# Projecting the output head group by head group, with attention units reordered head-major and mixed anew, in a decode attention kernel

## The chip, the cores and the metric

The kernel runs on one core of one Trainium2 chip. The metric is the device time of one execution in microseconds (us), as the median of several executions. Every kernel was timed in the same rounds, on the same chip, as the kernel before.

Engine names as in the profile: PE does matmuls (PEld loads their weights), DVE, ACT and POOL do elementwise work and reductions, SP issues the loads.

## The reference

Two independent attention layers (A and B), each with one query token per sequence. The outputs are concatenated.

```python
B, Sq, D = 8, 1, 1024
H, Sk, Dh = 32, 4096, 128
q = (x @ wq).reshape(B, Sq, H, Dh).transpose(0, 2, 1, 3)
scores = einsum("bhqd,bhkd->bhqk", q, k_cache) * (Dh ** -0.5)
p = softmax(scores, axis=-1)
o = einsum("bhqk,bhkd->bhqd", p, v_cache)
return o.transpose(0, 2, 1, 3).reshape(B, Sq, H * Dh) @ wo
```

The inputs are bfloat16. K and V of both layers are 1.07 GB; wq and wo add 8 MB each per layer. The scores are small, so the softmax is nearly uniform.

## The kernel before

A "unit" is one (batch, head) pair: 256 per layer, 512 in all, each with 1 MB of K and 1 MB of V. Scores are computed in one of two ways. A **P unit** transposes K on PE, has ACT evict it, and multiplies on PE (QK). A **D unit** multiplies K by the broadcast query on DVE and reduces there. `kinds` gives the mix; before it is "PD", alternating. Softmax and PV are the same for both kinds.

```python
def do_Dmul(u):          # D unit: DVE multiplies 128x4096 by 128x4096, both in SBUF
    m = plan.add("dve", lambda e: e.tensor_tensor(prod, K_sb[:, slot, :], qbc_broadcast, ALU.mult),   # cut
                 deps=[opK[u], opQbc[u], ...])
    opKfree[u] = m       # K's slot is free: SP may issue the load of unit u + 4
# ... cut: do_Dred reduces prod to 128x32 scores on DVE

def do_softmax(u):
    o1 = plan.add("dve", lambda e: e.tensor_reduce(rmax[:, u:u + 1], src, AX.X, ALU.max), deps=[opQK[u]])
    o2 = plan.add("pool", lambda e: e.partition_all_reduce(gmax[:, u:u + 1], rmax[:, u:u + 1], 128, ReduceOp.max), deps=[o1])
    o3 = plan.add("pool", lambda e: e.tensor_scalar(negb[:, u:u + 1], gmax[:, u:u + 1], -scale, None, ALU.mult), deps=[o2])
    o4 = plan.add("act", lambda e: e.activation(pT[:, u % PR, :], src, ACTF.Exp, bias=negb[:, u:u + 1],
                                                scale=scale, accum_out=rsum[:, u:u + 1]), deps=[o3, opPV.get(u - PR)])
    # ... cut: after each 8 units, one all-reduce (add) of their 8 sums on POOL -> Lall

def issue_K(u):          # on SP, in program order; V likewise, three units behind K
    deps = [opKfree.get(u - NK)] if u >= NK else []
    opK[u] = dma(K_sb[:, slot, :], caches[c][1][b, h]..., ("k", slot), deps)

# ... cut: after all 256 units of a layer, do_E1 normalises 128x256 outputs at once, then
# do_proj runs 2 x 32 matmuls (one per head and output half), and do_out stores the result
```

## Time and profile before

Each unit has one POOL all-reduce, which combines the maxima of the 128 partitions (`gmax<-rmax`), and then one small POOL operation that negates and scales the result (`negb<-gmax`), called negb below. The distance between two negb starts is thus the time of one unit.

| reading (profiled run, span 8085.1 us) | value |
|---|---|
| median time | 8086.3 us |
| negb starts, mean distance | 15.64 us, 511 times = 7994 us |
| gap from negb's end to the next all-reduce's start, mean | 7.21 us |
| from an all-reduce's start to its negb, mean (without the first unit) | 8.17 us |
| last negb to the end | 29.7 us |

First, the page: busy time by engine, then the chain that ended last.

```profile
PE 2556.2 (32%) x17812; PEld 1343.7 (17%) x17812; DVE 1790.5 (22%) x1043; ACT 1457.0 (18%) x1857; POOL 582.3 (7%) x1106
...
issue 74%; DVE 12%; POOL 7%; PE 5%; ACT 1%; POOLq 1%; DMA 0%; SPq 0%; DVEq 0%
```

No engine is busy for a third of the span, and three quarters of the chain is "issue", time that waits for nothing the profile shows. The page's groups (line, engine, operation, count, busy us, mean ns, idle time just before them) say whose time it is:

```profile
L406 POOL PARTITION_ALL_REDUCE gmax<-rmax x512 | 338.3, 661 | 3127.2 <-issue 1727.4
L408 POOL TENSOR_SCALAR negb<-gmax 128x1 f32<-128x1 f32 x512 | 133.2, 260 | 3851.0 <-issue 3851.0
```

POOL, 7% busy, stands before these two lines for 3127 + 3851 of 8085 us. The timeline of two units (start us, duration us, engine, line, operation; in brackets the idle time before) shows the rhythm. SPq lines are load issues.

```profile
4015.02 0.26 POOL L408 TENSOR_SCALAR negb<-gmax 128x1 f32<-128x1 f32 x1 [7.47 <-issue]
...
4020.00 0.33 SPq L131 DMA_DIRECT2D V_sb<-in_B_v_cache_dram  x1
...
4021.26 0.38 POOL L406 PARTITION_ALL_REDUCE gmax<-rmax  x1 [5.98 <-issue]
4021.31 2.29 DVE L384 TENSOR_TENSOR prod<-K_sb,qbc 128x4096 bf16<-128x4096 bf16 x1 [15.04 <-ACT qbc L370]
...
4025.11 0.33 SPq L131 DMA_DIRECT2D K_sb<-in_B_k_cache_dram  x1
4025.48 0.43 SPq L131 DMA_DIRECT2D V_sb<-in_B_v_cache_dram  x1
4025.96 0.43 SPq L131 DMA_DIRECT2D K_sb<-in_B_k_cache_dram  x1
4030.67 0.26 POOL L408 TENSOR_SCALAR negb<-gmax 128x1 f32<-128x1 f32 x1 [9.03 <-issue]
...
4038.09 0.38 POOL L406 PARTITION_ALL_REDUCE gmax<-rmax  x1 [7.16 <-DVE rmax L404]
```

All-reduce, 6 to 10 us of nothing, negb, 6 to 10 us of nothing, and so on, 512 times. The row maximum that an all-reduce needs was ready 7 to 28 us before POOL had finished the previous unit, in all but three units, so POOL does not wait for data. The releaser in the last bracket is inferred and is a coincidence: that maximum was not the one this all-reduce needed. POOL's reported spans are thus no measure of the time it takes here: they sum to 7% of the span, the distances between negb starts to 99%.

The projection is at the very end:

```profile
8055.33 0.26 POOL L408 TENSOR_SCALAR negb<-gmax 128x1 f32<-128x1 f32 x1 [6.78 <-issue]
...
8065.12 9.46 PE L489 MATMUL misc<-W_sb,on_sb 128*8 128x512 bf16 x32 [4.12 <-DVE on_sb L475]
...
8075.36 7.07 PE L489 MATMUL misc<-W_sb,on_sb 128*8 128x512 bf16 x32 [0.77 <-DVE orow L497]
8082.46 0.68 DVE L497 CAST orow<-misc 8x512 bf16<-8x512 f32 x1 [7.16 <-PE misc L489]
```

### The profile page before, as it was taken

To read this page: it belongs to the slowest core of one execution; us is meant where nothing else is said; L and a number is where in the kernel's file an instruction comes from. 1 tells how busy PE (TensorE), PEld (TensorE's weight loads), DVE (VectorE), ACT (ScalarE), POOL (GpSimd) and SP (SyncE) were. 2 spreads that over 40 slices of the span, in tenths; PEclk is the share of its full clock that TensorE was granted. 3 is DMA by queue.
4 is the path that set the end of the run, shared out by engine and by line. 5 is a ranking of instruction groups with operands and counts; after the bars stand their busy time and mean duration, and the time that the engine had idled before them with its cause. 6 is when DMAs were issued, how large, how long until landed. Compare 5 with 4: busy or idle time off the path is not lost.

```text
span 8085.1 us, 43421 instructions
## 1 busy us (share of the span) xinstructions
PE 2556.2 (32%) x17812; PEld 1343.7 (17%) x17812; DVE 1790.5 (22%) x1043; ACT 1457.0 (18%) x1857; POOL 582.3 (7%) x1106
## 2 busy tenths in 40 slices
PE   3333333232323232323333233333333333333333
PEld 2111111111111111111111111111111111111111
DVE  2222222222222222222222222222222222222221
ACT  1111111111111111111111111111111111111111
POOL 0000000000000000000000000000000000000000
PEclk6566666666666666666566566665666566666666
DMA  6333333333333333333343333333333333333331
GB/s 271 125 146 125 146 125 146 125 146 125 138 132 138 132 140 131 137 134 131 139 166 131 140 129 142 126 144 126 144 125 146 125 146 125 145 125 145 125 145 63
DMA packets 158470, 1110.20 MB, mean 137 GB/s; under 512 B 16928, under 2 KB 16928, under 8 KB 25152
## 3 DMA queue, kind: packets, MB, share of 16 engines
q1 hardware_dynamic: 158272, 1107.43, 35.3%
q8 instruction: 140, 2.29, 0.1%
q14 instruction: 58, 0.48, 0.0%
HBM read 1107.33 MB, written 0.03 MB: 137 GB/s over the span
## 4 chain that ended last, share of the span: by engine, by line
issue 74%; DVE 12%; POOL 7%; PE 5%; ACT 1%; POOLq 1%; DMA 0%; SPq 0%; DVEq 0%
DVE s_sb L396 10%; PE sc L334 4%; POOL gmax L406 4%; POOL negb L408 2%; POOL Lall L420 1%; ACT pT L410 1%; DVE prod L384 1%; DVE rmax L404 1%; POOLq L408 0%; PE misc L489 0%; DMA W_sb<-in_A_wq_dram 0%; PE misc L206 0%; PE sc L437 0%; POOLq L74 0%; POOLq L406 0%
## 5 line engine op out<-in xcount | busy, mean ns | idle before, releaser
L437 PE MATMUL sc<-V_sb,pT 128*4 128x512 bf16 x4096 | 1484.3, 527 | 4017.7 <-ACT accS L445 4007.6
L437 PEld LDWEIGHTS sc<-V_sb,pT 128*4 128x4 bf16 x4096 | 386.3, 104 | 4899.4 <-ACT accS L445 4160.0
L404 DVE TENSOR_REDUCE rmax<-sc 128x1 f32<-128x32 f32 x256 | 49.0, 191 | 5171.9 <-PE sc L334 5171.9
L396 DVE TENSOR_REDUCE s_sb<-prod 128x32 f32<-128x4096 bf16 x256 | 1128.7, 4409 | 0.5 <-DVE rmax L404 0.5
L311 ACT ACTIVATE KT_sb<-kt_all 128x4096 bf16<-128x4096 bf16 x256 | 917.3, 3583 | 8.5 <-PE kt_all L297 2.3
L334 PE MATMUL sc<-QB,KT_sb 128*128 128x64 bf16 x8192 | 469.0, 238 | 1403.7 <-ACT pT L410 1403.6
L410 ACT ACTIVATE pT<-s_sb,negb 128x32 bf16<-128x32 f32 x256 | 82.2, 321 | 4132.7 <-POOL negb L408 4132.7
L384 DVE TENSOR_TENSOR prod<-K_sb,qbc 128x4096 bf16<-128x4096 bf16 x256 | 585.3, 2286 | 891.5 <-ACT qbc L370 874.4
L334 PEld LDWEIGHTS sc<-QB,KT_sb 128*128 128x128 bf16 x8192 | 429.5, 128 | 1463.6 <-ACT pT L410 1463.6
L406 POOL PARTITION_ALL_REDUCE gmax<-rmax x512 | 338.3, 661 | 3127.2 <-issue 1727.4
L297 PE MATMUL kt_all<-ident,K_sb 128*128 128x128 f32 x4096 | 519.7, 282 | 3.8 <-ACT KT_sb L311 3.8
L410 ACT ACTIVATE pT<-sc,negb 128x32 bf16<-128x32 f32 x256 | 73.5, 287 | 2378.4 <-POOL negb L408 2378.4
L297 PEld LDWEIGHTS kt_all<-ident,K_sb 128*128 128x128 f32 x4096 | 459.4, 145 | 130.9 <-issue 130.9
L408 POOL TENSOR_SCALAR negb<-gmax 128x1 f32<-128x1 f32 x512 | 133.2, 260 | 3851.0 <-issue 3851.0
L445 ACT ACTIVATE accS<-sc 4x512 bf16<-4x512 f32 x512 | 300.4, 587 | 24.7 <-PE sc L437 6.9
L420 POOL PARTITION_ALL_REDUCE Lall<-rsum x64 | 110.9, 1733 | 492.0 <-issue 486.0
L458 PE MATMUL o_ps<-E,accS 128*128 128x4 bf16 x512 | 33.3, 169 | 60.3 <-ACT accS L445 54.0
L404 DVE TENSOR_REDUCE rmax<-s_sb 128x1 f32<-128x32 f32 x256 | 47.6, 186 | 8.9
L410 ACT ACTIVATION_READ_ACCUMULATOR pT<-sc,negb 128x1 f32 x256 | 49.3, 193 | 0.0
L370 ACT ACTIVATE qbc<-misc 128x512 bf16<-128x512 f32 x64 | 38.2, 597 | 58.6 <-PE misc L358 57.1
L410 ACT ACTIVATION_READ_ACCUMULATOR pT<-s_sb,negb 128x1 f32 x256 | 47.6, 186 | 0.0
L458 PEld LDWEIGHTS o_ps<-E,accS 128*128 128x128 bf16 x512 | 22.6, 102 | 132.2 <-ACT accS L445 132.2
(36 smaller groups left out, 156.3 us busy)
## 6 DMA issues: line engine op xcount, KB each, us to landing
K_sb<-in_A_k_cache_dram SPq DMA_DIRECT2D x256, 1024.0 KB, 8.6
V_sb<-in_A_v_cache_dram SPq DMA_DIRECT2D x256, 1024.0 KB, 6.8
K_sb<-in_B_k_cache_dram SPq DMA_DIRECT2D x256, 1024.0 KB, 8.3
V_sb<-in_B_v_cache_dram SPq DMA_DIRECT2D x256, 1024.0 KB, 6.8
W_sb<-in_A_wq_dram SPq DMA_DIRECT2D x8, 1024.0 KB, 12.0
W_sb<-in_B_wq_dram SPq DMA_DIRECT2D x8, 1024.0 KB, 17.0
W_sb<-in_A_wo_dram SPq DMA_DIRECT2D x8, 1024.0 KB, 14.3
W_sb<-in_B_wo_dram SPq DMA_DIRECT2D x8, 1024.0 KB, 14.9
```

The source lines that it names most:

```text
L297: return e.transpose(kt_all[:, g, tt * 128:(tt + 1) * 128], K32[:, slot, tp * 128:(tp + 1) * 128], ident32[:])
L311: return e.activation(KT_sb[:, pi % 2, lo * 1024:hi * 1024], ktb_all[:, lo:hi, :].rearrange("p g c -> p (g c)"), ACTF.Copy)
L334: return e.matmul(bank[:, 2 * tp:2 * tp + MW], KT_sb[:, pi % 2, tp * 256 + e_:(tp + 1) * 256:2], QB[:, c, (j * 2 + e_) * 2:(j * 2 + e_) * ...
L384: lambda e: e.tensor_tensor(prod[:].rearrange("p (t d) -> p t d", d=Dh), K_sb[:, slot, :].rearrange("p (t d) -> p t d", d=Dh), qbc[:, gi % ...
L396: lambda e: e.tensor_reduce(s_sb[:, di % SR, :], prod[:].rearrange("p (t d) -> p t d", d=Dh), AX.X, ALU.add),
L404: o1 = plan.add("dve", lambda e: e.tensor_reduce(rmax[:, u:u + 1], src, AX.X, ALU.max), deps=[opQK[u]], name=f"rmax{u}")
L406: o2 = plan.add("pool", lambda e: e.partition_all_reduce(gmax[:, u:u + 1], rmax[:, u:u + 1], 128, bass.bass_isa.ReduceOp.max), deps=[o1], ...
L408: o3 = plan.add("pool", lambda e: e.tensor_scalar(negb[:, u:u + 1], gmax[:, u:u + 1], -scale, None, ALU.mult), deps=[o2], name=f"negb{u}")
L410: o4 = plan.add("act", lambda e: e.activation(pT[:, u % PR, :], src, ACTF.Exp, bias=negb[:, u:u + 1], scale=scale, accum_out=rsum[:, u:u + ...
L420: o5 = plan.add("pool", lambda e: e.partition_all_reduce(Lall[:, u0:u1], rsum[:, u0:u1], 128, bass.bass_isa.ReduceOp.add), deps=[opExp[uu] ...
L437: return e.matmul(bank[32 * q4:32 * q4 + 4, 0:512], pT[:, u % PR, 4 * g:4 * g + 4], V_sb[:, slot, g * 512:(g + 1) * 512], start=(g == 0), ...
L445: a = plan.add("act", lambda e: e.activation(accS[32 * q4:32 * q4 + 4, ring, :], bank[32 * q4:32 * q4 + 4, 0:512], ACTF.Copy), deps=[op, o ...
```

## The change

The intent was to take the output projection off the end. Units run head by head (all 8 batches of head 0, then head 1), so that a head's outputs are complete early. Each head is normalised on its own, and the projection runs in nine pieces per layer (seven of four heads, one of three, one of one) that are accumulated in SBUF. The same diff also changes the mix of units from "PD" to "PDD", makes the last two units P units, moves the loads of the second wq and of wo to later units and the first computation of q behind the first unit's transposes, and lets the first V loads leave earlier.

```diff
-    kinds_pat = cfg.get("kinds", "PD")
+    kinds_pat = cfg.get("kinds", "PDD")
+    for u in range(max(0, NT - cfg.get("tail_p", 2)), NT):
+        kind[u] = "P"
 # ... cut
         def unit_src(u):
             c, j = divmod(u, N)
-            b, h = divmod(j, H)
+            h, b = divmod(j, B)
 # ... cut: do_E1 (all heads at once) becomes do_HE(c, h), one head
-        def do_proj(c, ph, wo_ops):
-            for h in range(H):
+        def do_piece(c, h0, h1, wo_ops, final):
+            for ph in range(NPH):
+                for h in range(h0, h1):
+                    # matmuls into misc, start at h0, stop at h1 - 1
+                if h0 == 0:   # DVE copies misc to oacc
+                else:         # DVE adds misc to oacc (to orow in the last piece)
 # ... cut: the schedule of q, wo and the pieces
```

More of the change, by code (lines that the diff above doesn't have):

```diff
@@ L43, in _build_kernel @@
     MW = cfg.get("MW", 64)
-    LB = cfg.get("LB", 8)
-    kinds_pat = cfg.get("kinds", "PD")
+    kinds_pat = cfg.get("kinds", "PDD")
     act_banks = cfg.get("act_banks", 4)
@@ L65, in _build_kernel @@
     assert D % PW == 0 and 2 * N <= 512
+    LB = B
     kind = [kinds_pat[u % len(kinds_pat)] for u in range(NT)]
+    for u in range(max(0, NT - cfg.get("tail_p", 2)), NT):
+        kind[u] = "P"
     p_units = [u for u in range(NT) if kind[u] == "P"]
@@ L101, in _build_kernel @@
         pT = sb("pT", [128, PR, T], BF16)
-        rl = sb("rl", [128, N], FP32)
+        rl = sb("rl", [128, 4, B], FP32)
+        oacc = sb("oacc", [B, NC, D], FP32)
         on_sb = sb("on_sb", [128, NC, H, B], BF16)
@@ L216, in q_compute @@
                 "dve",
-                lambda e: e.tensor_copy(
-                    qT_sb[:, c, 0:N].rearrange("p (b h) -> p h b", h=H),
-                    misc[:, 0:N].rearrange("p (h b) -> p h b", b=B)),
+                lambda e: e.tensor_copy(qT_sb[:, c, 0:N], misc[:, 0:N]),
                 deps=[last], name=f"q{c}_evac")
@@ L236, in _build_kernel @@
         op_q = [None] * NC
-        op_q[0] = q_compute(0, wq_ops)
         opKfree = {}
@@ L462, in do_EXT @@
                     deps = [opAcc[uu] for uu in range(u0, u0 + 4)] + [op_E4]
-                    if j == 0 and c > 0:
-                        deps.append(opE1[c - 1])
+                    deps += [v_ for v_ in list(opHE.values())[-2:]]
                 op = plan.add("pe", fn, deps=deps, name=f"EXT{u0}_{jj}")
@@ L467, in do_EXT @@
                 opExt[uu] = op
-        def do_E1(c):
-            u_last = (c + 1) * N - 1
-            a = plan.add("dve", lambda e: e.reciprocal(rl[:, 0:N], Lall[:, c * N:(c + 1) * N]),
-                         deps=[opAradd[uu] for uu in range(c * N, (c + 1) * N, LB)] + [opE1.get(c - 1)], name=f"E1a{c}")
-            b_ = plan.add(
-                "dve",
-                lambda e: e.tensor_tensor(
-                    on_sb[:, c, :, :].rearrange("p h b -> p b h"),
-                    o_ps[:, c * N:(c + 1) * N].rearrange("p (b h) -> p b h", h=H),
-                    rl[:, 0:N].rearrange("p (b h) -> p b h", h=H),
-                    ALU.mult),
-                deps=[a, opExt[u_last]], name=f"E1b{c}")
-            opE1[c] = b_
@@ L483, in _build_kernel @@
-        proj_ops = {}
-        def do_proj(c, ph, wo_ops):
-            last = None
-            for h in range(H):
-                def fn(e, h=h):
-                    return e.matmul(misc[0:B, 0:PW], on_sb[:, c, h, :], W_sb[:, h * D + ph * PW: h * D + (ph + 1) * PW],
-                                    start=(h == 0), stop=(h == H - 1))
-                deps = []
-                if h == 0:
-                    deps = [opE1[c], last_misc_reader[0]] + wo_ops
-                last = plan.add("pe", fn, deps=deps, name=f"P{c}_{ph}_{h}")
-            if ph == NPH - 1:
-                w_last_user[0] = last
-            ev = plan.add("dve", lambda e: e.tensor_copy(orow[0:B, c, ph * PW:(ph + 1) * PW], misc[0:B, 0:PW]),
-                          deps=[last], name=f"Pev{c}_{ph}")
-            last_misc_reader[0] = ev
-            proj_ops[(c, ph)] = ev
-            return ev
+        opHE = {}
@@ new lines, in _build_kernel, with do_HE @@
+        piece_last = {}
+        pieces_done = {c: 0 for c in range(NC)}
+        def do_HE(c, h):
+            u0 = c * N + h * B
+            ring = h % 4
+            a = plan.add("dve", lambda e: e.reciprocal(rl[:, ring, :], Lall[:, u0:u0 + B]),
+                         deps=[opAradd[u0], opHE.get((c, h - 4)) if h >= 4 else None], name=f"HEa{c}_{h}")
+            b_ = plan.add("dve", lambda e: e.tensor_tensor(on_sb[:, c, h, :], o_ps[:, u0:u0 + B], rl[:, ring, :], ALU.mult),
+                          deps=[a, opExt[u0 + B - 1]], name=f"HEb{c}_{h}")
+            opHE[(c, h)] = b_
@@ new lines, in do_piece, with fn @@
+        def do_piece(c, h0, h1, wo_ops, final):
+            for ph in range(NPH):
+                last = None
+                for h in range(h0, h1):
+                    def fn(e, h=h, ph=ph):
+                        return e.matmul(misc[0:B, 0:PW], on_sb[:, c, h, :], W_sb[:, h * D + ph * PW: h * D + (ph + 1) * PW],
+                                        start=(h == h0), stop=(h == h1 - 1))
+                    deps = []
+                    if h == h0:
+                        deps = [opHE[(c, hh)] for hh in range(h0, h1)] + [last_misc_reader[0]] + wo_ops
+                    last = plan.add("pe", fn, deps=deps, name=f"P{c}_{h0}_{ph}_{h}")
+                dst = orow[0:B, c, ph * PW:(ph + 1) * PW] if final else oacc[0:B, c, ph * PW:(ph + 1) * PW]
+                if h0 == 0:
+                    ev = plan.add("dve", lambda e, dst=dst: e.tensor_copy(dst, misc[0:B, 0:PW]),
+                                  deps=[last], name=f"Pev{c}_{h0}_{ph}")
+                else:
+                    ev = plan.add("dve", lambda e, dst=dst, ph=ph: e.tensor_tensor(dst, oacc[0:B, c, ph * PW:(ph + 1) * PW], misc[0:B, 0:PW], ALU.add),
+                                  deps=[last, piece_last.get(c)], name=f"Pev{c}_{h0}_{ph}")
+                last_misc_reader[0] = ev
+                if ph == NPH - 1:
+                    piece_last[c] = ev
+                    if final:
+                        w_last_user[0] = last
+            pieces_done[c] = h1
@@ L503, in do_out @@
         def do_out(c):
-            deps = [proj_ops[(c, ph)] for ph in range(NPH)]
-            return dma(out[:, 0, c * D:(c + 1) * D], orow[0:B, c, :], "o", deps, f"out{c}")
+            return dma(out[:, 0, c * D:(c + 1) * D], orow[0:B, c, :], "o", [piece_last[c]], f"out{c}")
         LAG_V = cfg.get("LAG_V", 3)
@@ L511, in _build_kernel, with piece_sizes @@
         PV_LAG_D = cfg.get("PV_LAG_D", 2)
-        assert SM_LAG_P >= QK_LAG and PV_LAG_P > SM_LAG_P or (PV_LAG_P >= SM_LAG_P)
-        IT_WQ_LOAD = {c: (c - 1) * N + cfg.get("q_load_at", 1) for c in range(1, NC)}
-        IT_Q_COMP = {c: (c - 1) * N + cfg.get("q_comp_at", min(6, N - 3)) for c in range(1, NC)}
-        IT_WO_LOAD = {c: c * N + cfg.get("wo_load_at", min(8, N - 1)) for c in range(NC)}
+        HE_DELAY = cfg.get("he_delay", 2)
+        PC_DELAY = cfg.get("pc_delay", 2)
+        OUT_DELAY = cfg.get("out_delay", min(24, N - 8))
         TAIL = max(PV_LAG_P, PV_LAG_D) + 1
-        IT_PROJ = {c: (c + 1) * N + TAIL for c in range(NC)}
-        for c in range(1, NC):
-            assert IT_WQ_LOAD[c] < IT_Q_COMP[c] < IT_WO_LOAD[c - 1] <= c * N + 1
-        for c in range(1, NC):
-            assert IT_WO_LOAD[c] > IT_PROJ[c - 1] + NPH - 1, (IT_WO_LOAD, IT_PROJ)
+        IT_WQ_LOAD = {c: cfg.get("q_load_at", min(10, max(1, N // 8))) + (c - 1) * cfg.get("q_step", min(24, max(2, N // 4)))
+                      for c in range(1, NC)}
+        IT_Q_COMP = {c: IT_WQ_LOAD[c] + cfg.get("q_comp_dly", min(12, max(1, N // 8))) for c in range(1, NC)}
+        IT_Q_COMP[0] = 0
+        IT_WO_LOAD0 = (max(IT_Q_COMP.values()) + cfg.get("wo_dly", min(12, max(1, N // 8)))) if NC > 1 else 2
+        def piece_sizes():
+            sizes = []
+            rem = H
+            while rem > 5:
+                sizes.append(4)
+                rem -= 4
+            if rem > 1:
+                sizes.append(rem - 1)
+            sizes.append(1)
+            return sizes
+        PSZ = piece_sizes()
+        assert sum(PSZ) == H
         pending_wq = {}
         wo_loaded = {}
-        out_ops = []
+        wo_iter = {}
+        piece_iter_last = {}
+        out_ops = {}
+        out_due = {}
         k_next = 0
         v_next = 0
-        n_iter = NT + TAIL + NPH
+        n_iter = NT + TAIL + 8
         QBC_AHEAD = cfg.get("qbc_ahead", 2)
@@ L531, in _build_kernel @@
         ext_done = 0
-        e1_done = 0
+        ext_iter = {}
+        he_done = {c: 0 for c in range(NC)}
+        he_iter = {}
         for it in range(n_iter):
+            last_it = (it == n_iter - 1)
             progressed = True
@@ L540, in _build_kernel @@
                     progressed = True
-                if v_next < NT and (v_next <= k_next - 1 - LAG_V or k_next >= NT) and (v_next < NV or (v_next - NV) in opPV):
+                vmax = (k_next - 1 - LAG_V) if (k_next < NT and k_next > NK) else NT
+                if v_next < NT and v_next <= vmax and (v_next < NV or (v_next - NV) in opPV):
                     issue_V(v_next)
@@ L548, in _build_kernel @@
             for c in range(NC):
-                if it == IT_WO_LOAD[c]:
-                    wo_loaded[c] = load_wo(c)
+                if c in wo_loaded:
+                    continue
+                ready = all(q is not None for q in op_q) and (c == 0 or (pieces_done[c - 1] == H))
+                if ready and it >= (IT_WO_LOAD0 if c == 0 else 0) and it >= wo_iter.get(c - 1, -100) + 1:
+                    if c == 0 or it >= piece_iter_last[c - 1] + NK + 4 or last_it:
+                        wo_loaded[c] = load_wo(c)
+                        wo_iter[c] = it
             while qbc_done < len(d_units):
@@ L560, in _build_kernel @@
                 do_EXT(ext_done + 3)
+                for uu in range(ext_done, ext_done + 4):
+                    ext_iter[uu] = it
                 ext_done += 4
-            while e1_done < NC and ext_done >= (e1_done + 1) * N and all(uu in opAradd for uu in range(e1_done * N, (e1_done + 1) * N)):
-                do_E1(e1_done)
-                e1_done += 1
+            for c in range(NC):
+                while he_done[c] < H:
+                    h = he_done[c]
+                    u1 = c * N + (h + 1) * B - 1
+                    if u1 >= ext_done or (c * N + h * B) not in opAradd:
+                        break
+                    final_head = (c == NC - 1 and h == H - 1)
+                    if not (final_head or it >= ext_iter[u1] + HE_DELAY or last_it):
+                        break
+                    do_HE(c, h)
+                    he_iter[(c, h)] = it
+                    he_done[c] += 1
+            for c in range(NC):
+                if c not in wo_loaded:
+                    continue
+                while pieces_done[c] < H:
+                    h0 = pieces_done[c]
+                    acc_ = 0
+                    for sz in PSZ:
+                        if acc_ == h0:
+                            break
+                        acc_ += sz
+                    h1 = h0 + sz
+                    if he_done[c] < h1:
+                        break
+                    final = (h1 == H)
+                    last_piece = final and c == NC - 1
+                    if not (last_piece or last_it or (it >= he_iter[(c, h1 - 1)] + PC_DELAY and it >= wo_iter[c] + NK + 6)):
+                        break
+                    do_piece(c, h0, h1, wo_loaded[c], final)
+                    piece_iter_last[c] = it
+                    if final:
+                        out_due[c] = it + (OUT_DELAY if c < NC - 1 else 0)
+            for c in range(NC):
+                if c in out_due and c not in out_ops and (it >= out_due[c] or last_it):
+                    out_ops[c] = do_out(c)
             if it < NT:
@@ L569, in _build_kernel @@
                     do_Dmul(it)
+            for c in range(NC):
+                if it == IT_Q_COMP[c]:
+                    wq_o = wq_ops if c == 0 else pending_wq.pop(c)
+                    op_q[c] = q_compute(c, wq_o)
             u = it - SM_LAG_P
@@ L581, in _build_kernel @@
                     do_PV(u)
-            for c in range(1, NC):
-                if it == IT_Q_COMP[c]:
-                    op_q[c] = q_compute(c, pending_wq.pop(c))
-            for c in range(NC):
-                for ph in range(NPH):
-                    if it == IT_PROJ[c] + ph:
-                        assert c in opE1
-                        do_proj(c, ph, wo_loaded[c])
-                        if ph == NPH - 1:
-                            out_ops.append(do_out(c))
         assert len(out_ops) == NC and k_next == NT and v_next == NT, (len(out_ops), k_next, v_next)
@@ L594, in _build_kernel @@
         assert qbc_done == len(d_units) and ext_done == NT
+        assert all(pieces_done[c] == H for c in range(NC))
         counts = {e: 0 for e in ENGINES}
```

## The prediction

> **What bounds the kernel now.** Not the projection, nor any engine by busy time (page, part 1: PE 32%, DVE 22%, ACT 18%, POOL 7%). In the chain of waits 74% is "issue" under POOL's lines L406 (all-reduce of the maximum) and L408 (negb). In the timeline POOL runs one strict sequence for each of 512 units: all-reduce, 7.2 to 9.3 us later negb, 5.9 to 9.5 us later the next all-reduce. negb starts are 15.64 us apart on average (least 13.3); 511 x 15.64 = 7994 of 8085 us. The row maximum an all-reduce needs was ready 7 to 25 us before POOL had finished the previous unit, in all but 3 units: POOL is never short of work. The instruction listing shows an extra unnamed POOL instruction before nearly every all-reduce and every negb[...].
>
> With no loads in flight (last units) a unit takes 13.3 us. The other 2.3 us are disturbance: K and V traffic, about 3 us per pair of units (estimate from gap differences), and multiplies of D units (L384, 2.29 us). In 93 of 255 gaps before a D unit's all-reduce the whole multiply lies inside; 72 of those all-reduces start 0.2 us after it ends, at 9.5 instead of 7.5 us. [...]
>
> **What the change does.** POOL's work stays: 512 all-reduces, 512 negb, 64 sums over 8, as many extra instructions.
> - Projection in pieces, the last of one head: today 29.7 us pass from last negb to end (projection 18); I expect 13. Gain 17 us.
> - The first q now stands behind unit 0's transposes on PE, so behind K's arrival: first all-reduce at 57 instead of 47.5 us. Loss 10.
> - POOL waited 43 us in three early units (one at the second q). Gain 20 to 30.
> - PD becomes PDD: fewer transposes, evictions, QK groups; 341 instead of 256 multiplies and reductions (4.41 us). DVE stays hidden; what counts is phase. QK of the next P unit now follows two PV groups, so I expect the two multiplies about 10 and 17 us after a P unit's exp, where all-reduces start at 6 and 20.7: mostly clear of each other. Load bursts come per three units instead of two. I estimate 15.0 to 15.5 us a unit.
> - Per-head normalisation, 16 pieces: hidden under 20 us of slack.
>
> **Prediction.** 511 x 15.2 + 57 + 13 + 15 = 7852, say 7860 us; 7690 to 8060 eight times in ten. Chances: faster by over 2% 0.57, same 0.38, slower 0.05. The named purpose, the projection, is worth some 20 us (0.25%); the rest is the mix of units.
>
> **What would show it.** Mean negb spacing near 15.2; fewer all-reduces starting 0.2 us after a multiply; last negb to end 13 us; first all-reduce near 57 us.
>
> **What would make it wrong.** Other phases: 85 more multiplies meet all-reduce starts (up to 2 us each, +170 us); [...] (spacing stays 15.6: 8060); or DVE stalls at the new normalisation starve POOL.

Passages are cut here, and from some expectations below. The clause cut before "(spacing stays 15.6: 8060)" named loads, now spread, that would disturb every gap. The sum stands whole, 511 x 15.2 + 57 + 13 + 15 = 7852. Its 15.2 is the estimate from the trace before (15.64 us a unit on average, 13.3 at the least).

## The result, and the profile after

The kernel after takes 8035.91 us in the median of 11 runs (8003.73 to 8066.68), the kernel before 8086.3 (15 runs). The ratio is 0.9942, 95% interval 0.9928 to 0.9956. It is faster by 0.6%, where 2.8% was predicted.

The same lines of the page after:

```profile
PE 2177.9 (27%) x13864; PEld 991.0 (12%) x13864; DVE 2394.5 (30%) x1367; ACT 1156.8 (14%) x1795; POOL 475.7 (6%) x1106
...
issue 54%; DVE 27%; PE 11%; POOL 4%; ACT 3%; POOLq 0%; DMA 0%; SPq 0%; DVEq 0%
...
L408 POOL TENSOR_SCALAR negb<-gmax 128x1 f32<-128x1 f32 x512 | 222.1, 434 | 3785.0 <-issue 3785.0
L406 POOL PARTITION_ALL_REDUCE gmax<-rmax x512 | 226.5, 442 | 3371.7 <-issue 3187.1
```

POOL's idle time before these two lines is 7157 us, before it was 6978. The chain now names DVE more often, because the chain is inferred from coincidences like the one above; POOL's sequence still fills the span. The chain's shares are therefore not what the argument should rest on.

The timeline over the end of one all-reduce and the next:

```profile
3965.13 0.38 POOL L406 PARTITION_ALL_REDUCE gmax<-rmax  x1 [5.97 <-DVE rl L475]
...
3965.23 2.29 DVE L384 TENSOR_TENSOR prod<-K_sb,qbc 128x4096 bf16<-128x4096 bf16 x1
...
3966.58 0.33 SPq L134 DMA_DIRECT2D K_sb<-in_B_k_cache_dram  x1
3966.95 0.43 SPq L134 DMA_DIRECT2D V_sb<-in_A_v_cache_dram  x1
3967.54 0.33 SPq L134 DMA_DIRECT2D K_sb<-in_B_k_cache_dram  x1
...
3967.91 0.66 SPq L134 DMA_DIRECT2D V_sb<-in_A_v_cache_dram  x1
...
3972.11 2.28 DVE L384 TENSOR_TENSOR prod<-K_sb,qbc 128x4096 bf16<-128x4096 bf16 x1
3972.42 2.07 POOL L408 TENSOR_SCALAR negb<-gmax 128x1 f32<-128x1 f32 x1 [6.92 <-issue]
3974.42 0.33 SPq L134 DMA_DIRECT2D K_sb<-in_B_k_cache_dram  x1
...
3984.01 0.38 POOL L406 PARTITION_ALL_REDUCE gmax<-rmax  x1 [9.52 <-issue]
```

Two things are to be seen. The negb at 3972.42 takes 2.07 instead of 0.26 us: a multiply began 0.3 us earlier, and negb ended 0.1 us after the multiply did (as all 49 negbs of this trace that take over 0.4 us do). And after a burst of five loads within 8 us the next gap is 9.5 us instead of 6.0. The windows view (the gap's bounds, its length, busy us and count of each engine, granted clock, share of the load engines, GB/s) of that gap and of the quiet gap at 3931 to 3937:

```profile
3931.30:3937.30 6.00, 0.00 (x0) 0.00 (x0) 0.00 (x0) 4.00 (x3) 0.02 (x2) 0.50 0.14 59
...
3974.50:3984.00 9.50, 0.00 (x0) 0.00 (x0) 4.53 (x2) 3.88 (x3) 0.00 (x0) 0.50 0.63 265
```

The load engines are 63% busy in the long gap and 14% in the short one. DVE is busy too (4.53 us), so the two lines alone do not tell which of the two stretched it.

The end answers as intended:

```profile
8022.77 0.26 POOL L408 TENSOR_SCALAR negb<-gmax 128x1 f32<-128x1 f32 x1 [7.09 <-issue]
...
8029.85 0.38 PE L486 MATMUL misc<-W_sb,on_sb 128*8 128x512 bf16 x1 [1.24 <-DVE on_sb L477]
...
8031.42 0.68 DVE L497 TENSOR_TENSOR orow<-oacc,misc 8x512 bf16<-8x512 f32 x1 [0.47 <-PE misc L486]
```

Where the 51 us between the two profiled spans (8085.1 and 8034.0) lie:

| part of the span | before | after | difference |
|---|---|---|---|
| start to first negb | 61.0 | 65.0 | +4.0 |
| 511 distances between negb starts | 7994.3 (15.64 each) | 7957.8 (15.57 each) | -36.5 |
| last negb to the end | 29.7 | 11.2 | -18.5 |

And inside the 511 distances: the gaps from negb to the next all-reduce grew by 51 us in sum, the stretches from an all-reduce to its negb shrank by about 177, and negb itself grew from 133 to 222 us.

### The profile page after: what moved, and what is told of

Read it like the earlier page. It is cut to its first block, busy times and chain, and to the rows that moved or that the text cites. A ratio compares the mean times of both kernels' runs of the same rounds, so it can differ in the third digit from the quotient of the medians.

```text
span 8034.0 us, 35966 instructions
## 1 busy us (share of the span) xinstructions
PE 2177.9 (27%) x13864; PEld 991.0 (12%) x13864; DVE 2394.5 (30%) x1367; ACT 1156.8 (14%) x1795; POOL 475.7 (6%) x1106
## 4 chain that ended last, share of the span: by engine, by line
issue 54%; DVE 27%; PE 11%; POOL 4%; ACT 3%; POOLq 0%; DMA 0%; SPq 0%; DVEq 0%
DVE s_sb L396 17%; DVE prod L384 9%; PE sc L437 7%; PE sc L334 3%; POOL gmax L406 2%; ACT accS L445 2%; POOL negb L408 1%; ACT pT L410 1%; DVE rmax L404 1%; PE misc L358 0%; PE misc L486 0%; POOL Lall L420 0%; POOLq L408 0%; PE o_ps L458 0%; DMA K_sb<-in_A_k_cache_dram 0%
## 5 line engine op out<-in xcount | busy, mean ns | idle before, releaser
L396 DVE TENSOR_REDUCE s_sb<-prod 128x32 f32<-128x4096 bf16 x340 | 1502.8, 4420 | 11.7
L384 DVE TENSOR_TENSOR prod<-K_sb,qbc 128x4096 bf16<-128x4096 bf16 x340 | 776.0, 2282 | 1.4 <-ACT qbc L370 1.4
L311 ACT ACTIVATE KT_sb<-kt_all 128x4096 bf16<-128x4096 bf16 x172 | 614.4, 3572 | 30.6 <-PE kt_all L297 28.6
L408 POOL TENSOR_SCALAR negb<-gmax 128x1 f32<-128x1 f32 x512 | 222.1, 434 | 3785.0 <-issue 3785.0
L406 POOL PARTITION_ALL_REDUCE gmax<-rmax x512 | 226.5, 442 | 3371.7 <-issue 3187.1
L297 PE MATMUL kt_all<-ident,K_sb 128*128 128x128 f32 x2752 | 357.7, 286 | 22.2 <-DMA K_sb<-in_A_k_cache_dram 15.6
L297 PEld LDWEIGHTS kt_all<-ident,K_sb 128*128 128x128 f32 x2752 | 321.8, 149 | 30.8 <-DMA K_sb<-in_A_k_cache_dram 15.7
L334 PE MATMUL sc<-QB,KT_sb 128*128 128x64 bf16 x5504 | 239.4, 210 | 8.2 <-ACT pT L410 8.2
L334 PEld LDWEIGHTS sc<-QB,KT_sb 128*128 128x128 bf16 x5504 | 223.8, 110 | 9.3 <-ACT pT L410 8.3
L420 POOL PARTITION_ALL_REDUCE Lall<-rsum x64 | 27.3, 426 | 387.0 <-issue 381.1
```

What stands on the lines that cost most here:

```text
L297: return e.transpose(kt_all[:, g, tt * 128:(tt + 1) * 128], K32[:, slot, tp * 128:(tp + 1) * 128], ident32[:])
L311: return e.activation(KT_sb[:, pi % 2, lo * 1024:hi * 1024], ktb_all[:, lo:hi, :].rearrange("p g c -> p (g c)"), ACTF.Copy)
L334: return e.matmul(bank[:, 2 * tp:2 * tp + MW], KT_sb[:, pi % 2, tp * 256 + e_:(tp + 1) * 256:2], QB[:, c, (j * 2 + e_) * 2:(j * 2 + e_) * ...
L384: lambda e: e.tensor_tensor(prod[:].rearrange("p (t d) -> p t d", d=Dh), K_sb[:, slot, :].rearrange("p (t d) -> p t d", d=Dh), qbc[:, gi % ...
L396: lambda e: e.tensor_reduce(s_sb[:, di % SR, :], prod[:].rearrange("p (t d) -> p t d", d=Dh), AX.X, ALU.add),
```

## The experiments

Sixteen runs. "Spacing" is the mean distance of negb starts, "gap before" runs from negb's end to the next all-reduce's start, "gap after" from an all-reduce's start to its negb. All three come from each run's timeline; the gap after leaves out the first unit.

| run | kernel | median us | ratio to before | spacing | gap before | gap after |
|---|---|---|---|---|---|---|
| | before | 8086.3 | 1 | 15.64 | 7.21 | 8.17 |
| | after | 8035.9 | 0.9942 | 15.57 | 7.31 | 7.83 |
| E1 | before, mix PDD | 8076.6 | 1.0007 | 15.62 | 7.24 | 7.95 |
| E2 | after, mix PD | 8031.3 | 0.9947 | 15.57 | 6.99 | 8.32 |
| E3 | after, P units only | 7336.2 | 0.9087 | 14.22 | 6.21 | 7.75 |
| E4 | after, negb on ACT | 2760.9 | 0.3420 | | | |
| E5 | after, multiply cut | 7944.0 | 0.9845 | 15.39 | 7.49 | 7.64 |
| E6 | after, loads cut | 7273.2 | 0.9013 | 14.08 | 6.15 | 7.51 |
| E7 | before, multiply cut | 7866.7 | 0.9749 | 15.19 | 7.06 | 7.87 |
| E8 | before, loads cut | 7256.4 | 0.8994 | 14.02 | 6.16 | 7.60 |
| E9 | after, loads held to all-reduce | 8230.2 | 1.0178 | 15.97 | 6.26 | 9.24 |
| E10 | before, loads held to all-reduce | 8492.2 | 1.0504 | 16.43 | 6.16 | 10.01 |
| E11 | P only, loads held to negb | 8962.1 | 1.1079 | 17.42 | 9.67 | 7.49 |
| E12 | before, negb on ACT | 2715.3 | 0.3358 | | | |
| E13 | E9, loads 2.2 us later still | 7284.9 | 0.9037 | 14.11 | 6.25 | 7.45 |
| E14 | P only, loads held to all-reduce | 8474.0 | 1.0516 | 16.45 | 6.24 | 9.95 |
| E15 | as E2, one look | 8006.8 | | 15.52 | 6.97 | 8.29 |
| E16 | after, mix PD, negb on ACT | 2701.9 | 0.3352 | | | |

### Which half of the change did it: E1 and E2

The first theory (LOADS) said that K and V traffic disturbs POOL by a fixed amount per unit, whatever the mix (2.2 us, an estimate; the mean spacing before, 15.64 us, is 2.3 over the least, 13.3), the rival (DVE) that multiplies and reductions do.

```diff
E1  -    kinds_pat = cfg.get("kinds", "PD")      E2  -    kinds_pat = cfg.get("kinds", "PDD")
E1  +    kinds_pat = cfg.get("kinds", "PDD")     E2  +    kinds_pat = cfg.get("kinds", "PD")
```

> The kernel before with only the unit mix changed (PD to PDD); correct result. Theory LOADS [...]: spacing of negb stays 15.5 to 15.7 us, time 8050 to 8100 us. Theory DVE (multiplies and reductions on DVE hold POOL; more D units cost, phases give back): spacing moves by over 0.15 us, time outside 8010 to 8160. If the mix alone explains what the change gained, 8040 to 8060.

> The kernel after with the old unit mix (PD), so only head-major order and the projection in pieces remain; correct result. LOADS: spacing as before, 15.6 us, and only start, early waits and end shorter: 8086 minus 20 to 50 = 8036 to 8066 us. DVE: as before in the middle too, so the same; but then it must lie above the kernel after only if the mix PDD is a gain (E1 under 8060).

The mix alone is worth nothing (1.0007, interval 0.9994 to 1.002); its time and spacing are where LOADS put them. Order and pieces alone are worth 0.9947 (0.9935 to 0.9959), which is the whole change; the time is 5 us under what LOADS said. So the part from which the prediction took nearly all its gain gave none by itself. The two parts are not independent, though. In E2's trace 16 all-reduces, about one per piece, start only 0.1 us or so after their own row maximum, 12 us instead of about 6 after the previous negb: there POOL did wait for data, some 93 us in sum. In the kernel after only two do. With the order and the pieces, the mix PDD therefore does save something, which is lost again elsewhere. One of these waits in E2:

```profile
1615.33 0.26 POOL L408 TENSOR_SCALAR negb<-gmax 128x1 f32<-128x1 f32 x1 [6.80 <-issue]
...
1627.24 0.17 DVE L404 TENSOR_REDUCE rmax<-sc 128x1 f32<-128x32 f32 x1
...
1627.55 0.38 POOL L406 PARTITION_ALL_REDUCE gmax<-rmax  x1 [11.96 <-DVE rmax L404]
```

E15 is E2's kernel once more and agrees.

> Order and pieces of the change with the old mix PD once more, one look only, as a check of E2: 7990 to 8060 us.

### P units only: E3

```diff
-    kinds_pat = cfg.get("kinds", "PDD")
+    kinds_pat = cfg.get("kinds", "P")
-        QK_LAG = cfg.get("QK_LAG", 2)
-        SM_LAG_P = cfg.get("SM_LAG_P", 3)
+        QK_LAG = cfg.get("QK_LAG", 1)
+        SM_LAG_P = cfg.get("SM_LAG_P", 2)
```

> The kernel after with P units only (no multiply, no 4.4 us reduction; QK one unit later and softmax two units later instead of two and three, to keep it free of races); correct result. LOADS: spacing 15.0 to 15.6 us, time 7750 to 8050. DVE: spacing falls to 13.3 plus at most 1, time 7000 to 7400.

7336 us, outside LOADS' range and inside DVE's. Read alone, this is a verdict for DVE. But the edit changed two things: it took away DVE's work, and it moved the moments at which the loads leave. The next runs separate them.

### What the gaps on POOL are: E4 and E12

```diff
-            o3 = plan.add("pool", lambda e: e.tensor_scalar(negb[:, u:u + 1], gmax[:, u:u + 1], -scale, None, ALU.mult),
+            o3 = plan.add("act", lambda e: e.activation(negb[:, u:u + 1], gmax[:, u:u + 1], ACTF.Copy, scale=-scale),
```

If the gaps come from the alternation of all-reduce and tensor_scalar on POOL, they vanish here.

> The kernel after with negb computed on ACT instead of POOL, so that POOL runs all-reduces alone; correct result. [...]the kernel bound elsewhere (DVE 2390 us busy, PE 2180, loads 35% of the span = 2800 us), time 3000 to 4500 us. If instead the gap is the all-reduce's own work or its dispatch, the time falls by less than 8%, to 7500 or more.

> The kernel before with negb on ACT, to compare with E4: what the change is worth once POOL does not bound. Loads bind at about 402 GB/s as in E4, mix PD has DVE at 1790 us: time 2750 to 2900, the change being worth the serial end (20 to 30 us, 1%) and little else. If the mix or the pieces cost something once POOL is out of the way, this is the faster of the two.

One line moved to another engine, the result still correct, and the time falls to 0.342 (after) and 0.336 (before). (E4's expectation said 3000 to 4500 us and E12's 2750 to 2900; both came out faster.) With only all-reduces on POOL the gaps are gone: of the 1776.1 us that POOL idles before L406 in E4's page, 1775.6 end with a row maximum from DVE. In the timeline of E4:

```profile
1400.12 0.35 POOL L406 PARTITION_ALL_REDUCE gmax<-rmax  x1 [4.56 <-DVE rmax L404]
...
1401.19 0.20 ACT L408 ACTIVATE negb<-gmax 128x1 f32<-128x1 f32 x1
```

From the all-reduce's start to negb it takes 1.1 us here (2.6 on average, 0.4 at the least); it was 7 to 10. So the gaps belong to the alternation of two kinds of POOL instruction, not to the all-reduce. The trace of the kernel before says the same: after 63 of its all-reduces another all-reduce follows directly, and starts 0.3 to 2.4 us later. What POOL does in the gaps is not shown. The trace has an extra pair of POOL instructions, MODIFY_POOL_CONFIG, at each alternation (`--source L408` counts 1024, two for each negb), and in E4 only two are left at the all-reduce (its page counts 33918 instructions, 2048 fewer than the 35966 of the kernel after). But these take 0.08 us each at negb and 0.01 at the all-reduce, and nothing in the profile accounts for the rest of the 6 to 7 us.

Both kernels are now bound by the loads: the load queue's share of 16 engines is 97.6% in E4 and 98.6% in E12, 402 and 409 GB/s. Here the kernel before is the faster one, by 1.8% (0.342 to 0.3358).

### Multiply and loads, one at a time: E5 to E8

```diff
E5, E7: the multiply works on 2 of 32 blocks (in the first D unit on all)
-  e.tensor_tensor(prod[...], K_sb[...], qbc[...], ALU.mult)
+  e.tensor_tensor(prod[...][:, 0:2, :], K_sb[...][:, 0:2, :], qbc[...], ALU.mult)
E6, E8: after the first loads, K and V loads bring 256 of 4096 columns
+  wd = T * Dh if u < NK else 256
+  opK[u] = dma(K_sb[:, slot, 0:wd], ...[:, 0:wd], ...)
```

> The kernel after with each D unit's multiply cut to 2 of 32 blocks (wrong result on purpose), reductions kept. Spacing of negb with P units only was 14.22 us, with the kernel after 15.57. Theory MULTIPLY (only the two-input multiply holds POOL): spacing 14.1 to 14.5, time 7290 to 7480. Theory REDUCTION (the 4.4 us reduction holds it too): spacing at least 14.9, time over 7680.

> The kernel after with every K and V load after the first ones cut to one sixteenth (wrong result on purpose), all engines' work kept. If loads cost nothing but through DVE's phase: 15.3 to 15.7 us a unit, about 8030. If loads alone account for what P units only leave over 13.3 us (0.9 us a unit): 14.5 to 14.8, about 7500 to 7620. [...]: 13.3 to 13.8, 6870 to 7120.

> The kernel before with the multiply cut the same way (wrong result on purpose). MULTIPLY: spacing 14.1 to 14.5, 7290 to 7510, like the kernel after with the same cut (its 85 more D units then cost nothing). REDUCTION: 14.9 to 15.3, 7680 to 7900.

> The kernel before with K and V loads cut to one sixteenth (wrong result on purpose). Same three readings: 15.4 to 15.7 us a unit (loads innocent, 8000 to 8090), 14.5 to 14.9 (loads alone cost 0.9, 7500 to 7700), 13.3 to 13.8 (DVE disturbs only with loads in flight, 6870 to 7120).

(The last range of E6's expectation belongs, as in E8's, to DVE's operations disturbing POOL only while loads are in flight.) E6 and E8 give wrong results. E5 and E7 compute wrong scores too, but passed the comparison, since the softmax is nearly uniform.

MULTIPLY falls: both kernels stay at 15.2 us and more. Cutting the loads, with all of DVE's work kept, brings both to 14.0 to 14.1. In E6 the gap before a P unit's all-reduce, which still holds a whole 4.4 us reduction (3.8 us on average inside it), is 6.18 us; in the kernel after, with the loads, it is 9.7. So E3's verdict is turned round: reductions cost nothing without loads. These two runs also missed all three readings written down for each: 14.08 and 14.02 us lie between "loads alone" and "DVE only with loads". The trace of the kernel after also tells reductions and multiplies apart: 70 of its negbs lie wholly within a reduction and all take 0.26 us; 53 start within a multiply and take 2.09 us in the median.

The multiply's share can be read by difference: 15.64 - 15.19 = 0.45 us a unit before, 15.57 - 15.39 = 0.18 after. This compares kernels whose phases also shift, so it is an estimate. A third more multiplies cost less than half as much. With multiplies out of the way the new kernel is slower per unit (15.39 against 15.19). The loads' share by difference is 15.64 - 14.02 = 1.62 us a unit before and 15.57 - 14.08 = 1.49 after. The two pairs do not fit together as a sum: the first says that loads cost the new kernel more than the old, the second that they cost it less. Multiplies and loads meet in the same gaps, so removing one changes what the other costs.

Sorting the gaps before by how long the load engines were busy in their first 6 us, from the transfer records of the two profiled runs:

| loads busy in the first 6 us | before: gaps, mean length | after: gaps, mean length |
|---|---|---|
| under 3.0 us | 264, 6.12 us | 350, 6.11 us |
| 3.0 to 5.7 us | 214, 8.23 us | 8, 8.45 us |
| nearly all of it | 33, 9.40 us | 153, 10.01 us |

In the after kernel's long gaps the all-reduce starts 2.7 us (median) after the last of the loads that were in flight at negb's end has landed. Before, loads of two units left together; after, loads of three units do, because K's slots are freed in bunches by PE and DVE. Fewer gaps meet loads, but those are met for longer. This is still a correlation. It suggested the third theory, BURSTS: what counts is when loads are issued. A gap before an all-reduce would end only after the loads in flight have landed, and loads issued six at a time would cost about 4 us per three units (an estimate: 10.01 less 6.11 us in the table).

### Moving the loads: E9, E10, E11

The edit adds a wait, so it can only delay loads: `pool_seq` lists the all-reduces (E9, E10) or the negbs (E11) in POOL's order.

```diff
E9, E10:
             deps = [opKfree.get(u - NK)] if u >= NK else []
+            if u - 6 >= 0:
+                deps.append(pool_seq[u - 6])
E11 (on E3's kernel): u - 5, and K is planned one unit later
-                if k_next < NT and k_next <= it + NK - 1 and ...
+                if k_next < NT and k_next <= it + NK - 2 and ...
```

> The kernel after with one wait added: K's load number u (and with it V's number u-3) is not issued before the all-reduce six places earlier in POOL's order has run, so that one K and one V leave at the start of each all-reduce, and none are in flight when POOL turns from negb to the next all-reduce; correct result. Theory BURSTS [...]: all gaps negb to all-reduce near 6.1 us, spacing 14.1 to 14.6, time 7270 to 7540. Rival DVE (the gaps of 10 us come from reductions and multiplies that fall into them): spacing stays 15.3 to 15.7, about 7900 to 8090.

> The kernel before with the same wait added; correct result. BURSTS: gaps before D units' all-reduces fall from 8.3 to about 6.2 us, but multiplies, which cost this mix about 200 us, stay: spacing 14.4 to 15.0, time 7430 to 7730. DVE: 15.4 to 15.7, 7930 to 8090.

> The kernel with P units only (E3) and K's load u held until the negb five places earlier[...]; correct result, no multiply and no reduction of products on DVE anywhere. BURSTS: gaps negb to all-reduce rise from 6.2 to 7.5 to 9 us, spacing 15.5 to 17, time 8000 to 8750, slower than E3 by over 8%. DVE: no D units, so 14.2 us a unit as in E3, 7290 to 7400.

E11 is the strongest single run: no product multiply or reduction on DVE, the same bytes, and 22% more time than E3 from the moment of issue alone (8962 against 7336), more than the 8000 to 8750 us that BURSTS said. Holding the loads back did not starve POOL instead: 14 of E11's all-reduces start within 0.6 us after their row maximum, in E3 18. Two units of it, POOL and SP:

```profile
4007.58 0.38 POOL L409 PARTITION_ALL_REDUCE gmax<-rmax  x1 [9.72 <-issue]
4014.86 0.26 POOL L411 TENSOR_SCALAR negb<-gmax 128x1 f32<-128x1 f32 x1 [6.91 <-issue]
...
4015.21 0.33 SPq L134 DMA_DIRECT2D K_sb<-in_A_k_cache_dram  x1
4015.58 0.43 SPq L134 DMA_DIRECT2D V_sb<-in_A_v_cache_dram  x1
...
4024.40 0.38 POOL L409 PARTITION_ALL_REDUCE gmax<-rmax  x1 [9.27 <-issue]
```

E9 and E10 missed, and fit neither theory. They did to the gap before what BURSTS said (6.26 and 6.16 us), but the gap after rose to 9.24 and 10.01 us, and both kernels became slower. I had moved the loads from one gap to the other. In E9 they left about 0.4 us after the all-reduce's start; in E3, where both gaps are short, at 1.9 us:

```profile
3999.43 0.38 POOL L406 PARTITION_ALL_REDUCE gmax<-rmax  x1 [5.94 <-issue]
4001.30 0.33 SPq L134 DMA_DIRECT2D K_sb<-in_B_k_cache_dram  x1
4001.67 0.43 SPq L134 DMA_DIRECT2D V_sb<-in_B_v_cache_dram  x1
4006.86 0.26 POOL L408 TENSOR_SCALAR negb<-gmax 128x1 f32<-128x1 f32 x1 [7.06 <-issue]
4012.99 0.38 POOL L406 PARTITION_ALL_REDUCE gmax<-rmax  x1 [5.87 <-issue]
```

### The right moment: E13 and E14

```diff
E13 (on E9): the list holds the last of two copies on ACT that start after the all-reduce
+            od = o2
+            for _ in range(2):
+                od = plan.add("act", lambda e: e.activation(x_sb[:, 0, :], x_sb[:, 0, :], ACTF.Copy),
+                              deps=[od, op_xT, pool_seq[-1] if pool_seq else None])
-            pool_seq.append(o2)
+            pool_seq.append(od)
E14 (on E11): the all-reduce instead of negb
-            pool_seq.append(o3)
+            pool_seq.append(o2)
```

MOMENT, a hypothesis, said that loads issued at the very start of a gap lengthen it and loads issued later in it do not (0.4 us after the all-reduce's start in E9, 1.9 in E3).

> E9 with the loads issued about 2.3 us later still (two small copies on ACT, otherwise idle then, stand between the end of the all-reduce and the issue); correct result. In E3 loads issued 1.9 us after an all-reduce's start left both gaps short. MOMENT [...]: gaps after the all-reduce fall from 9.2 to 7.4 to 7.9 us, gaps before it stay near 6.1, spacing 14.1 to 14.6, time 7270 to 7540. LOADS COST ANYWHERE: spacing stays over 15.3, time over 7900.

> E11 with K's load held until the end of an all-reduce instead of the end of negb (P units only, no multiply or product reduction on DVE); correct result. MOMENT: gaps after the all-reduce 9.5 to 10.2 us, before it 6.0 to 6.3, spacing 15.8 to 16.6, time 8130 to 8550, between E3 (7336) and E11 (8962). If E9 and E10 were slow through DVE: as E3, 7290 to 7450.

Both land where MOMENT put them. E13 keeps every multiply, every reduction and every byte of the change, adds two useless copies and one wait per unit, and is 9.1% faster than the change itself (0.9037 against 0.9942 of before). Its POOL and SP lines:

```profile
4005.76 0.38 POOL L409 PARTITION_ALL_REDUCE gmax<-rmax  x1 [5.98 <-issue]
4006.16 2.14 ACT L413 ACTIVATE x_sb<-x_sb 8x1024 bf16<-8x1024 bf16 x2 [5.37 <-POOL gmax L409]
4008.38 0.33 SPq L134 DMA_DIRECT2D K_sb<-in_B_k_cache_dram  x1
4008.75 0.43 SPq L134 DMA_DIRECT2D V_sb<-in_B_v_cache_dram  x1
4013.23 0.26 POOL L415 TENSOR_SCALAR negb<-gmax 128x1 f32<-128x1 f32 x1 [7.10 <-issue]
...
4019.73 0.38 POOL L409 PARTITION_ALL_REDUCE gmax<-rmax  x1 [6.24 <-issue]
```

Issued 2.6 us after the all-reduce's start, K and V leave both gaps short, even where they are still in flight when the next gap begins: the 347 gaps of E13 with 1.5 to 3 us of loads in their first 6 us have a mean of 6.09 us. The traces before, after and of E13 agree on how the length of the gap goes with the landing of the loads in flight at negb's end: landed within 3 us, the gap is 6.0 to 6.2 us in nearly all cases; between 4 and 5 us, about 8; between 6 and 7, 9 to 10; later than that, no more than about 10. E14 shows that E9 and E10 were not slow for DVE's sake: with P units only, the gap after is 9.95 us in the same place.

What E3, E11, E13 and E14 show is the dependence on the moment. By what mechanism the loads lengthen a gap is not shown.

### What the change is worth when POOL does not bound: E16

```diff
-    kinds_pat = cfg.get("kinds", "PDD")
+    kinds_pat = cfg.get("kinds", "PD")
 # and negb on ACT, as in E4
```

> Order and pieces of the change with the old mix PD and negb on ACT: loads bind at about 410 GB/s as in E12 (ratio to before 0.3358), and the serial end of the projection is gone: 2660 to 2710 us, ratio 0.330 to 0.335. If E4's 1.7% over E12 came from pieces or order and not from the mix PDD (DVE 87% busy), 2740 to 2780.

2701.9 us, ratio 0.3352 (0.3346 to 0.3358), against 0.3358 (0.3353 to 0.3363) for E12. This is the best version, correct, and 99.2% of its span is load time at 411 GB/s. But E12 is not distinguishable from it: order and pieces win 0.2%, which is within the noise. E4, which differs from E16 by the mix alone, is 2% slower: E4's loss against E12 therefore came from the mix PDD, which makes DVE 87% busy (67% in E12 and E16), and not from the pieces.

## Why the prediction was right or wrong

- **The bound: right.** POOL's sequence of 512 all-reduces and negbs set the time, at 6% busy; E4 shows it, with a ratio of 0.342.
- **The end: right.** 29.7 us became 11.2 (predicted 13).
- **The start: right in direction.** The first all-reduce moved from 47.5 to 52.3 us (predicted 57).
- **The early waits: wrong in effect.** The first 20 distances shrank by 22 us in sum, but the 40 after them grew by 19, where the first wo is now loaded. The gain was moved, not won.
- **The multiplies: right in effect, by luck in the phase.** "Mostly clear of each other" held for the all-reduces: those that start within 0.3 us after a multiply's end fell from 65 to none (the prediction, with a wider limit, counted 72 before). But the phase was not the predicted one. The next two multiplies start 21.2 and 28.1 us (medians) after a P unit's exp, not 10 and 17, while the all-reduces start at 6.1 and 20.4, as predicted. So the first multiply begins just after an all-reduce, and the second where a negb falls: 49 negbs now take over 0.4 us, up to 2.35; before, none did. By E5 and E7 the multiplies' cost fell from 0.45 to 0.18 us a unit (an estimate, see there).
- **The loads: the step that failed.** The prediction said only "Load bursts come per three units instead of two", and priced this at nothing on the way to "I estimate 15.0 to 15.5 us a unit". The two traces show what it cost: the gaps before an all-reduce that met loads for 3 us or more of their first 6 fell from 247 to 161, but their mean length rose from 8.4 to 9.9 us. Over the 6.11 us of a quiet gap they lost 561 us in sum before and 615 after. So the gaps before grew by 51 us where the estimate needed them to shrink, and took more than half of the 88 us that the stretches from an all-reduce to the end of its negb gained; 36 us are left. That the loads do this, and not DVE, is shown by E13 (and, without any multiplies, by E11): the same multiplies, reductions and bytes, but loads at another moment, and 15.57 us become 14.11. How many of the missing microseconds belong to the loads alone is not settled: E5 and E7 say 0.20 us a unit more than before, E6 and E8 say 0.13 less, because the two disturbances share gaps.
- **The mis-sized term:** 511 x 15.2 was predicted, 511 x 15.57 measured, 189 us more. The predicted time 7860 missed 8036 by 176; the range 7690 to 8060 held it, the gain did not. Among the three things named that would make it wrong, "spacing stays 15.6: 8060" is what came, and its cause was loads, but not "now spread": they were bunched.
- **Why I did not see it.** The packed transfer records, read directly, count from a zero that lies 11.1 us (before) and 10.7 us (after) ahead of the first instruction, which is the timeline's zero, and while predicting I laid one over the other without the shift. (The `--windows` and page views allow for it.) I therefore saw loads in the wrong gaps, and "about 3 us per pair" for K and V could not be tied to a place. A load's issue line in the timeline, which needs no shift, would have shown the bunches.

(The prediction's "16 pieces" should have read 18, and the smallest gap of the trace before is 5.78 us rather than 5.9; neither mattered.)

What stays open is what POOL does between its two kinds of instruction, and why loads issued at the wrong moment cost 2 to 4 us and no more; the profile has no record of it. Open too is why E2 reaches the change's spacing of 15.57 us with other gaps (6.99 and 8.32 us against 7.31 and 7.83); its 16 waits for data are a part of it, and nothing here shows why the two sums are equal. E13's late loads were not tried on the kernel before, so whether the change would win or lose once loads leave at a good moment is not known.

## What to carry to other kernels

When an engine is hardly busy and yet sets the time, measure the spacing of its instructions, and ask what it alternates between: moving one tiny operation to another engine was worth 66% here, against 0.6% for a rewritten projection. Work that is moved off the critical path also moves the loads that it releases, so before pricing a new mix of work as phase luck, list when each buffer comes free and which stretch of the bottleneck the loads will then fall on. And when one edit removes two suspects at once, as E3 did, the verdict is worth nothing until each has been removed alone.
